# Memory attention and a one-expert MoE on one core: column sums as eight small products, a maximum in pieces, looser holds for VectorE's steps, the last tile in halves, smaller transfers

## The chip, the cores and the metric

One core of one Trainium2 chip. The metric is the device time of one execution, in microseconds (us), as the median of the runs shown. Engines: PE is TensorE (PEld its weight loads), DVE is VectorE, ACT is ScalarE, POOL is GpSimd, SP is SyncE, which here does nothing but issue DMAs. SPq and ACTq are the DMA issues on the queues of SP and ACT.

## The reference

```python
# q, k, v: (8, 8, 576, 64); phi: (8, 8, 576, 32)
a = softmax(phi, axis=2)                        # over the 576 tokens
k_m, v_m = a^T @ k, a^T @ v                     # (b, h, 32, 64)
attn = softmax(q @ k_m^T / 8)                   # over the 32 memories
x = (attn @ v_m), heads side by side            # (4608, 512)
logits = x @ w_gate + modality_bias[modality_id]
e = argmax(logits); g = softmax(logits)[e]
out = g * (relu(x @ w1[e]) @ w2[e])             # 8 experts, 512 -> 1024 -> 512
```

## The kernel before

The kernel guesses that all tokens go to one expert (the preferred one of the first token's bias), works everything out for that expert and checks the guess at the end; only if a token belongs elsewhere does a slow path run (it does not here). The 576 tokens of each of 8 batches are laid out as 64 rows by 9 columns; heads stand in two groups (`NG`) of four (`HG`).

For each batch b there is an attention part and an expert part.

The attention part, by its stage names: `max` (the maximum of phi over the 9 columns, on VectorE: `fold`, four operations that halve the width, for batches 1 to 7; a reduction over a strided view, L306, for batch 0), `top` (the maximum over the partitions), `exp` (subtract on VectorE at L368, exponent on ScalarE), `sums` (the sum over the columns, on POOL for batches 1 to 7), `kv` (`kv_products`: 72 products of 64 by 32 tiles, L403, then at L408 one product of 128 by 128 that sums over the partitions of each group by means of the 0/1 matrix `sides`; then the division), `kvT` (turned), `qt` (four turns of q, L539, on VectorE), `s` (scores, L548; L566 for batch 0), then the steps `e` (the turn out of PSUM L593, maximum L597, subtract L599, exponent L601), `n` (sum L609, reciprocal, multiply L619, turn L625), `xu` and `x` (the softmax weights split into an upper and a lower part, xah/xbh on ScalarE and xal/xbl on VectorE, L659 and L662), `l` (logits, L679 and L684), `g` (gates, L698 to L708) and `others`. The steps are made for two parts: the first four columns (xa) and the other five (xb). For odd batches `a_split` also saves xa and xb to DRAM, for the slow path.

The expert part: `vw` (the values times w1, L732, split into vwh by ScalarE, L153, and vwl by VectorE, L154), `h` (the hidden layer: for each of 8 slices six products, L779, into one PSUM bank; then `relu`: hh on ScalarE, L792, and the remainder hl on VectorE, L796) and `o` (the output tiles: 24 products of 512 columns each, L816; then the gate on ScalarE, L829, into one of two buffers `ob`, and the store, L837 or L841). The kinds of the hidden stages are h0 (first part, 0.72 us of TensorE each), h1 and h3 (second part of even and of odd batches, 0.9 us).

PSUM has four banks `pe` in a ring, for `h`, `vw` and `o`, and two pairs for the attention part. A hidden product waits for the `hl` that read the bank four allocations earlier.

What order the work has on every engine is settled by `weave` while the program is built: it keeps two lists, attention and experts, each in a fixed order, and takes in turn the stage that is ready by a model of costs (`TAKES`: TensorE's time and a chain such as "D1.5 A0.7" for VectorE 1.5 us, then ScalarE 0.7; T is VectorE at a time when POOL must be idle). An attention stage also has a due value, and is not taken before the experts' `progress` has reached it. Progress counts an output stage of 0.69 us as 0.69, a hidden stage at 0.35 and `vw` at 0.5 of its time. `BATCH` is the progress of a batch, 30.9. An attention stage with VectorE work is moreover held until

```python
ra = max(ra, free["D"] - (HOLD[ex[0][1]] - work if ex and ex[0][1] in HOLD else 3.5))
```

where `free["D"]` is when the model has VectorE free and `work` what the stage adds: with the next expert stage of kind h0, h1 or h3 it is taken only once VectorE's backlog and its own work stay within `HOLD`, else within 3.5 us. The engines then run their queues in that order, each waiting on semaphores.

The first 25 us are written out by hand in `plan_first`, with products on zeros (`warm`, `nothing`) in some places. From there on, `plan_memory`, `plan_turns` and `plan_steps` put the attention stages of each batch in the list; the due values of batch b start at `at0 = (b - 1) * BATCH - AHEAD - EARLIER`.

All loads and stores go through SP's queue in the order of the program: keys and values of batch b+1 once batch b's `kv` has been issued (`more_keys`), q of batch b+2 after the scores of batch b, in 16 DMAs of 72 KB that are issued one at each hidden or output stage (`load_some`, L195).

## Time and profile before

| | |
|---|---|
| median of 3 runs | 389.69 us (389.62 to 389.97) |
| the profiled execution | 389.69 us |
| its span in the profile | 387.9 us |
| PE busy | 375.3 us (97%) |
| DVE busy | 244.7 us (63%) |
| ACT busy | 141.3 us (36%) |
| POOL busy | 45.8 us (12%) |
| DMA | 56.89 MB in 91307 packets |
| products for output tiles, L816 | 864, 116.3 + 112.4 + 110.3 us busy |
| products on small tiles for keys and values, L403 and L408 | 1008 and 14, 15.7 and 2.7 us busy |

Busy times of PE overlap, since matmuls are pipelined: the time from one start to the next is shorter than the duration of one. The rows of a timeline give the start, the duration (of a run of equal instructions from the first start to the last end), the engine and line, what is written and read, how many, and in brackets how long the engine sat idle before and what ended that.

### The profile page before, as it was taken

The numbers are of one execution on the slowest core, as the hardware profiler recorded it, in microseconds if no ns is written. First come the engines' busy times: TensorE is split into PE (matmuls) and PEld (weight loads), VectorE is DVE, ScalarE is ACT, GpSimd is POOL, SyncE is SP. The second block draws the span as 40 slices with busy tenths as digits, with TensorE's granted clock in tenths as the row PEclk, the third lists the DMA queues.
The fourth block names the chain that finished last, engine by engine and source line by source line (L and its number), as shares of the span: only waits on it lengthen the run. The fifth ranks groups of instructions, "written<-read, shape, count | busy, mean of one in ns | idle before, by whom it ended". The sixth has DMA issues, their size and how long they took to land.

```text
span 387.9 us, 9645 instructions
## 1 busy us (share of the span) xinstructions
PE 375.3 (97%) x3891; PEld 303.3 (78%) x3893; DVE 244.7 (63%) x613; ACT 141.3 (36%) x327; POOL 45.8 (12%) x116
## 2 busy tenths in 40 slices
PE   6899999999999999999999999999999999999993
PEld 3577976889779886788879887798868878698982
DVE  4787756895786389836786476864887467750400
ACT  2382524425234243433433334323443325241410
POOL 4347030023000400030000300003000200000000
PEclk9999999999999999999999999999999999999997
DMA  8998679875761397639712397614411011531111
GB/s 300 379 394 183 103 140 344 225 210 150 243 120 42 94 298 184 208 82 276 119 34 56 75 300 126 255 28 119 182 29 42 15 30 27 198 102 32 28 36 55
DMA packets 91307, 56.89 MB, mean 147 GB/s; under 512 B 69236, under 2 KB 74356, under 8 KB 91252
## 3 DMA queue, kind: packets, MB, share of 16 engines
q1 hardware_dynamic: 90976, 55.87, 51.4%
q8 instruction: 33, 0.54, 0.6%
q10 hardware_dynamic: 276, 0.30, 0.2%
q14 instruction: 22, 0.18, 0.2%
HBM read 37.28 MB, written 18.87 MB: 145 GB/s over the span
## 4 chain that ended last, share of the span: by engine, by line
PE 85%; DVE 4%; SPq 4%; DMA 3%; ACT 1%; issue 1%; ACTq 0%
PE pe L816 47%; PE pe L779 24%; PE pair L403 4%; PE pe L732 3%; DMA q_sb<-in_q_dram 3%; SPq L195 3%; PE pair L548 2%; PE pair L679 1%; SPq L178 1%; DVE vwl L154 1%; PE pair L148 1%; PE pair L732 1%; PE pair L408 1%; DVE xbl L662 0%; ACT ob L829 0%
## 5 line engine op out<-in xcount | busy, mean ns | idle before, releaser
L816 PE MATMUL pe<-w2h,hh 128*128 128x512 f32 x288 | 116.3, 404 | 0.0
L816 PE MATMUL pe<-w2h,hl 128*128 128x512 f32 x288 | 112.4, 390 | 0.0
L816 PE MATMUL pe<-w2l,hh 128*128 128x512 f32 x288 | 110.3, 391 | 0.0
L796 DVE SCALAR_TENSOR_TENSOR hl<-pe,hh 128x256 fp32r<-128x256 f32 (+2 forms) x158 | 58.3, 392 | 43.1 <-ACT hh L792 42.3
L816 PEld LDWEIGHTS pe<-w2h,hh 128*128 128x128 f32 x288 | 54.1, 188 | 19.8 <-issue 9.7
L792 ACT ACTIVATE hh<-pe 128x256 fp32r<-128x256 f32 (+2 forms) x158 | 53.4, 362 | 41.6 <-PE pe L779 41.2
L816 PEld LDWEIGHTS pe<-w2l,hh 128*128 128x128 f32 x288 | 54.0, 188 | 11.8
L816 PEld LDWEIGHTS pe<-w2h,hl 128*128 128x128 f32 x288 | 54.2, 188 | 9.6
L829 ACT ACTIVATE ob<-pe,gates 128x512 f32<-128x512 f32 x36 | 24.6, 687 | 73.4 <-PE pe L816 48.1
L779 PE MATMUL pe<-xbh,vwh 128*128 128x320 f32 x128 | 40.3, 315 | 0.1
L779 PE MATMUL pe<-xbh,vwl 128*128 128x320 f32 x128 | 39.6, 309 | 0.0
L779 PE MATMUL pe<-xbl,vwh 128*128 128x320 f32 x128 | 39.6, 309 | 0.0
L779 PE MATMUL pe<-xah,vwh 128*128 128x256 f32 x124 | 35.2, 287 | 1.5 <-DVE hl L796 0.7
L779 PE MATMUL pe<-xal,vwh 128*128 128x256 f32 x124 | 35.0, 284 | 0.3 <-DVE xal L662 0.3
L779 PE MATMUL pe<-xah,vwl 128*128 128x256 f32 x124 | 34.9, 283 | 0.0
L337 POOL COPY ts<-tm 32x4 f32<-32x4 f32 x24 | 4.8, 199 | 198.8 <-DVE tm L329 198.1
L779 PEld LDWEIGHTS pe<-xah,vwh 128*128 128x128 f32 x124 | 23.6, 191 | 4.2 <-ACT xah L648 1.6
L779 PEld LDWEIGHTS pe<-xbh,vwh 128*128 128x128 f32 x128 | 24.0, 188 | 1.7 <-issue 0.9
L779 PEld LDWEIGHTS pe<-xbl,vwh 128*128 128x128 f32 x128 | 24.1, 188 | 0.3
L779 PEld LDWEIGHTS pe<-xal,vwh 128*128 128x128 f32 x124 | 23.7, 191 | 0.8 <-DVE xal L662 0.5
L779 PEld LDWEIGHTS pe<-xbh,vwl 128*128 128x128 f32 x128 | 24.0, 188 | 0.0
L779 PEld LDWEIGHTS pe<-xah,vwl 128*128 128x128 f32 x124 | 23.7, 191 | 0.0
(173 smaller groups left out, 430.0 us busy)
## 6 DMA issues: line engine op xcount, KB each, us to landing
kv_sb<-in_k_dram SPq DMA_DIRECT2D x8, 1152.0 KB, 7.2
kv_sb<-in_v_dram SPq DMA_DIRECT2D x8, 1152.0 KB, 9.7
out_dram<-ob SPq DMA_DIRECT2D x64, 128.0 KB, 2.4
q_sb<-in_q_dram SPq DMA_DIRECT2D x112, 72.0 KB, 2.8
ph<-in_phi_dram SPq DMA_DIRECT2D x7, 576.0 KB, 4.3
raw<-in_moe_w_dram SPq DMA_DIRECT2D x2, 1024.0 KB, 6.4
raw<-in_moe_w_dram SPq DMA_DIRECT2D x1, 1280.0 KB, 10.2
out_dram<-ob SPq DMA_DIRECT2D x4, 256.0 KB, 2.1
```

What stands on the lines that cost most here:

```text
L148: nc.tensor.transpose(dst, src, ident[:rows, :rows])
L154: nc.vector.tensor_tensor(l, src, h.bitcast(F32), op=ALU.subtract)
L195: nc.sync.dma_start(*later.pop(0))
L337: nc.gpsimd.tensor_copy(ts_[BL * a:BL * (a + 1)], live["tm"][BL * o:BL * (o + 1)])
L403: nc.tensor.matmul(live["kvp"][M * j:M * (j + 1), g], lhsT=pe[half, j, c * M:(c + 1) * M], rhs=kv_sb[half, :, j, c * D:(c + 1) * D], start ...
L548: nc.tensor.matmul(sc[g][M * j:M * (j + 1), a, 0:QC * BL], lhsT=kvT[b][rows, 0, M * j:M * (j + 1)], rhs=qT[rows, j, a], start=True, stop=T ...
L732: nc.tensor.matmul(pvs[g][M * j:M * (j + 1), :], lhsT=vT[b][rows, j, :], rhs=raw1[rows, j, cols], start=True, stop=not more, tile_position ...
L779: nc.tensor.matmul(ph[:, 0:n], lhsT=(vl if k == 2 else vh)[:, g, cols], rhs=xl if k == 1 else xh, start=(g == k == 0), stop=(g == NG - 1 a ...
L792: nc.scalar.activation(hs[0][:, f, h0:h0 + p1 - p0], live["ph", f][:, p0:p1], AF.Relu)
L796: nc.vector.scalar_tensor_tensor(hl, live["ph", f][:, p0:p1], 0.0, hh.bitcast(F32), op0=ALU.max, op1=ALU.subtract)
L816: nc.tensor.matmul(po, lhsT=tile_columns(hl if n == 1 else hh, f, t), rhs=(w2l if n == 2 else w2h)[:, f, :], start=(f == n == 0), stop=(f ...
L829: nc.scalar.activation(ob, po, AF.Copy, scale=gate_of(b, t))
```

## The change

- Idle products: one before and two after the subtraction of batch 0's maximum go (1 of 1, 2 of 4), and three before the second group's hidden products (3 of 3).
- In `kv_products` the one product with `sides` becomes eight with a column of ones, on the same 64 by 32 tiles as the products before it; the two groups' sums then lie in two banks. `sides` and its four memsets go.
- The maximum of batch 1: instead of `fold`, a strided reduction of heads 0 and 1 (`m2`), put before batch 0's second scores, one of head 2 before the step `n` of batch 0's second part, and one of head 3 between `xu` and `x` of that part (`m1`).
- `HOLD` rises from 1.9, 2.4, 2.2 to 2.2, 3.0, 2.7. `EARLIER` is 0 instead of -4 for batch 3 (its steps fall due 4 earlier than before) and -6 instead of 0 for batch 7 (6 later).
- The very last output tile: its two halves of 256 columns go through ScalarE and VectorE into two buffers, and are stored by SP and by ACT.
- The loads of keys and values of batches 1 to 7 are made in two column halves each. The saved copies of xa and xb lie in DRAM column by column, so that each piece is 1 KB instead of 4 or 5 KB.

```diff
-    sides = const.tile([P, NG], F32, name="sides")
-    xa_dram = [[dram.tile([P, NG * RA * P], ...
-    xb_dram = [[dram.tile([P, NG * RB * P], ...
+    xa_dram = [[dram.tile([RA, P, NG * P], ...
+    xb_dram = [[dram.tile([RB, P, NG * P], ...
+    def flat(x, n):
+        return x.rearrange("p i g c x -> p (i g c x)").rearrange("p (n y) -> p n y", n=n)
     def load_kv(b, t):
-        nc.sync.dma_start(kv_sb[:, t], halves((k, v)[t], b))
+        src = halves((k, v)[t], b)
+        pieces = 2 if b else 1
+        for i in range(pieces):
+            cols = slice(i * (QC * D // pieces), (i + 1) * (QC * D // pieces))
+            nc.sync.dma_start(kv_sb[:, t, :, cols], src[:, :, cols])
+    def heads_max(b, js):
+        if js.start == 0:
+            live["top", b] = wk.tile([P, HG, M], F32, name="top")
+        src = phs[b].rearrange("p j (c m) -> p j m c", m=M)
+        nc.vector.tensor_reduce(live["top", b][:, js], src[:, js], axis=AX.X, op=ALU.max)
     def kv_products(b):
-        live["psum"] = pk[:, 0, 2 * D:2 * D + NG]
+        live["psum"] = pk[:, :, 2 * D]
...
-        nc.tensor.matmul(live["psum"], lhsT=sums.rearrange("p j m -> p (j m)"), rhs=sides, start=True, stop=True)
+        for j in range(HG):
+            for g in range(NG):
+                half = slice(QP * g, QP * (g + 1))
+                nc.tensor.matmul(
+                    pk[M * j:M * (j + 1), g, 2 * D:2 * D + 1], lhsT=sums[half, j], rhs=ones_c[half],
+                    start=True, stop=True, tile_position=(QP * g, M * j),
+                )
     def a_split(b, part, step=None):
...
-                nc.sync.dma_start(d.bitcast(F32), x.rearrange("p i g c x -> p (i g c x)").bitcast(F32))
+                nc.sync.dma_start(d.bitcast(F32).rearrange("n p x -> p n x"), flat(x, n).bitcast(F32))
     def store(b, t):
         def finish(po):
+            if b == B - 1 and t is None:
+                rows = out[S * (b - 1):S * (b + 1)].rearrange("(p c) d -> c p d", c=QC)[QC - 1]
+                first, second = slice(0, DM // 2), slice(DM // 2, DM)
+                obs = [wk.tile([P, DM], F32, name="ob", bufs=2)[:, 0:DM // 2] for _ in range(2)]
+                nc.scalar.activation(obs[0], po[:, first], AF.Copy, scale=gate_of(b, t))
+                nc.vector.tensor_scalar(obs[1], po[:, second], gate_of(b, t), None, op0=ALU.mult)
+                nc.sync.dma_start(rows[:, first], obs[0])
+                nc.scalar.dma_start(rows[:, second], obs[1])
+                return
# TAKES
+        "m1": (0.0, "D0.55"), "m2": (0.0, "D1.1"),
-        "kv": (2.6, "D0.4 A0.7"),
+        "kv": (2.5, "D0.4 A0.7"),
# plan_memory
-            ("max", [], mem_max, 0.0),
+            *((("max", [], mem_max, 0.0),) if b > 1 else ()),
# plan_first
-        nothing(1)
         add(("exp", 0), "first exp", [("top", 0)], mem_exp, 0)
-        nothing(4)
+        nothing(2)
...
         add(("n", 0, 0, 1, 1), "n2", [], first_weights, 1, 1)
-        nothing(3, "pe")
...
         turns(1, 1, 27.2)
+        add(("max", 1, 0), "m2", [], heads_max, 1, slice(0, 2), floor=26.5)
# plan_steps
+        if b == 0:
+            names = [x[0] for x in todo]
+            for j, before in ((3, ("x", 0, 1)), (2, ("n", 0, 1, 0))):
+                todo.insert(names.index(before), (("max", 1, j - 1), "m1", [], heads_max, (1, slice(j, j + 1))))
+            todo += [(("max", 1), "nothing", [("max", 1, 2)], lambda: None, ())]
...
-    AHEAD, EARLIER, SPREAD = (5.8, 5.0), {3: -4.0}, 0.55
+    AHEAD, EARLIER, SPREAD = (5.8, 5.0), {7: -6.0}, 0.55
-        HOLD = {"h0": 1.9, "h1": 2.4, "h3": 2.2}
+        HOLD = {"h0": 2.2, "h1": 3.0, "h3": 2.7}
```

## The prediction

> **What bounds the kernel now.** I read the page first, then the table of busy times by stretch, then the waits of TensorE, then the timeline around each wait.

> ```profile
> span 387.9 us, 9645 instructions
> PE 375.3 (97%) x3891; PEld 303.3 (78%) x3893; DVE 244.7 (63%) x613; ACT 141.3 (36%) x327; POOL 45.8 (12%) x116
> ...
> 0.00:10.00 10.00, 7.03 (x141) 3.73 (x146) 4.82 (x11) 3.03 (x6) 4.04 (x34) 1.00 0.83 303
> 10.00:20.00 10.00, 8.80 (x253) 5.49 (x244) 7.97 (x26) 3.14 (x11) 2.94 (x13) 1.00 1.08 380
> 20.00:30.00 10.00, 9.69 (x92) 7.91 (x90) 8.31 (x20) 9.36 (x23) 4.79 (x4) 1.00 1.05 395
> 168.00:380.00 212.00, 212.00 (x1982) 174.04 (x1981) 122.16 (x308) 73.60 (x174) 14.82 (x31) 1.00 0.37 101
> ```

> The columns after the stretch are its length, then PE, PEld, DVE, ACT, POOL, the granted clock, the DMA share and GB/s. TensorE bounds the kernel: from 168 us to 380 us it has no gap at all, at full clock, so there only work taken from TensorE itself can shorten the run. Idle TensorE lies in the first 30 us (2.97+1.20+0.31 = 4.5 us), in the tail, and at two places between, which the waits name and the timeline of TensorE shows:

> ```profile
> 67.65 0.39 PE L779 MATMUL pe<-xah,vwh 128*128 128x256 f32 x1 [0.46 <-ACT xah L659]
> 68.38 0.39 PE L779 MATMUL pe<-xal,vwh 128*128 128x256 f32 x1 [0.34 <-DVE xal L662]
> 163.06 0.39 PE L779 MATMUL pe<-xah,vwh 128*128 128x256 f32 x1 [0.74 <-DVE hl L796]
> ```

> The bracket is the idle time just before and what ended it: a hidden product (L779) waits 0.80 us for batch 1's split of the weights and 0.74 us for VectorE's `hl` of batch 3. The sum below is made against the profiled execution, 389.69 us: 387.9 us of span and 1.79 us around it. It equals the median of the three runs.

> **Idle products.** One, two and three products of 512 columns go.

> ```profile
> 9.26 2.19 PE L422 MATMUL pair<-kv_sb,exp 64*64 64x128 f32 x72
> 23.09 0.50 PE L779 MATMUL pe<-xah,vwh 128*128 128x256 f32 x2 [0.26 <-ACT xah L648]
> 11.17 0.29 DVE L385 TENSOR_TENSOR sums<-sums,t2top 128x128 f32<-128x128 f32 x1
> 12.74 0.71 DVE L539 STREAM_TRANSPOSE q_sb<-q_sb 128x512 f32<-128x512 f32 x1 [0.31 <-DMA q_sb<-in_q_dram]
> ```

> The one stands before L361, which waits for VectorE anyway. The two stand before the first keys (9.26 to 11.45 us); an earlier start there ends at VectorE's sums all the same (11.46 us), and behind those the DVE queue stands until q has landed (12.74 us). The three stand before L779 at 23.09 us, which waits for ScalarE's xah even with them. All six: 0; at best -0.2 us if the keys' start counts (9.26 back to about 9.1, when the first exponents are there). If the idling lowered the clock, the products from 23.09 to 27.5 us would take twice as long, over 4 us; but the rows above grant 1.00 through 4.5 us of idling, so this gets 0.02, within rival 2. The four memsets of `sides` go from POOL, which waits for the token ids' load behind them: 0.

> **Sums as eight products.** For batches 1 to 7 the 128 by 128 product L408 becomes eight of 64 by 32, each issued as two instructions (L403's 72 products are 144 instructions).

> ```profile
> 131.84 2.25 PE L403 MATMUL pair<-kv_sb,exp 64*32 64x128 f32 x144
> 134.01 0.38 PE L408 MATMUL pair<-sides,sums 128*128 128x2 f32 x2
> 134.26 0.48 PE L816 MATMUL pe<-w2h,hh 128*128 128x512 f32 x1
> L403 PE MATMUL pair<-kv_sb,exp 64*32 64x128 f32 x1008 | 15.7, 271 | 0.0
> L433 PE MATMUL pair<-ones_c,sums x8: 193/204/214, 11.5 to 11.6; 64*64 64x1 f32 x8
> 11.51 0.29 PE L433 MATMUL pair<-ones_c,sums 64*64 64x1 f32 x8
> ```

> L408 holds TensorE from 134.01 to 134.26: 0.25 us. L403's last instruction starts at 131.84+2.25-0.27 = 133.82, so its 144 stand 13.8 ns apart, and 0.19 us go by before L408, a change of tile shape. That change stays, only later: the gain is small. The new instructions resemble L433 most (f32, one column): eight in 0.29 us less one of 0.204 us, so 12.3 ns apart; sixteen are 0.20 us. The shape change then follows an instruction of 204 instead of 271 ns and should be shorter by up to 0.07 us. Per batch 0.05 to 0.12 us; I take 0.08, times 7: **-0.55**. Bounds: at L403's 13.8 ns with an unchanged gap -0.2; at half of L433's spacing, as eight tiles share the array where it has four, and with the shorter gap -1.5. A loss would need over 16 ns apart. [...]

> **Maximum of batch 1 in pieces.** The fold's four operations go, three reductions come.

> ```profile
> 42.17 0.66 DVE L294 TENSOR_TENSOR t2top<-ph 128x512 f32<-128x512 f32 x1
> 43.65 0.29 DVE L298 TENSOR_TENSOR top<-top,ph 128x128 f32<-128x128 f32 x1
> L306 DVE TENSOR_REDUCE top<-ph 128x64 f32<-128x576 f32 x2 | 2.2, 1118 | 4.5 <-DMA ph<-in_phi_dram 4.5
> 31.15 0.91 DVE L593 STREAM_TRANSPOSE a<-pair 128x320 f32<-128x320 f32 x2 [1.85 <-PE pair L566]
> 35.56 0.82 DVE L609 TENSOR_REDUCE sa<-a 128x20 f32<-128x640 f32 x1 [0.73 <-ACT a L601]
> 39.55 0.82 DVE L662 TENSOR_TENSOR xbl<-aT,xbh 128x640 fp32r<-128x640 f32 x1 [0.85 <-ACT xbh L659]
> ```

> The fold takes 42.17 to 43.94, 1.77 us between the gates of batch 0 and the first `hl` of its second part. By L306 two heads cost 1.12 us and one head 0.56 (half). The pair stands before the scores of 31 us, where DVE idles 1.85 us; the two single ones stand before L609 and L662, where it idles 0.73 and 0.85 us for ScalarE. All three are covered. What they add is a need: phi of batch 1 by about 29 us.

> ```profile
> L175 SPq DMA_DIRECT2D ph<-in_phi_dram x7: 373/392/1452, 17.3 to 216.3; - x7
> DMA to landing us min/median/max: 3.7/4.1/10.0
> ```

> Issued at 17.3 with at most 10.0 us to land: 27.3 us. If it were later, the piece would hold up the `hl` behind it on DVE.

> **VectorE's work held back later (HOLD), and due times.** A step waits until VectorE's backlog plus the step is below HOLD. In the second part of batch 0 the planner's backlog after each h1 stage is 0.45+0.52 = 0.97 us, and the exponent step's VectorE cost 1.5: 2.47, over 2.4 and under 3.0. So today that step stands behind all eight `hl`, and after the change among them.

> ```profile
> 49.66 1.41 DVE L368 TENSOR_TENSOR exp<-ph,pair 128x640 f32<-128x640 f32 x2
> 60.89 0.78 DVE L593 STREAM_TRANSPOSE a<-pair 128x256 f32<-128x256 f32 x2 [3.19 <-PE pair L548]
> ```

> With the fold gone and the hold raised, L368 can run at about 46 us instead of 49.66; then come ScalarE's exponent, POOL's sums, keys and values, scores: L593 at about 57 instead of 60.89, and xah and xal 3 to 4 us before L779 asks for them. The two waits (0.46+0.34) go: **-0.80**. Next late there is nothing that I see: the values' weights are made on TensorE right before, and their remainder is wanted only by the fifth hidden product.

> ```profile
> 156.51 1.29 DVE L154 TENSOR_TENSOR vwl<-pe,vwh 128x512 fp32r<-128x512 f32 x2 [1.74 <-ACT vwh L153]
> 160.88 0.68 DVE L294 TENSOR_TENSOR t2top<-ph 128x512 f32<-128x512 f32 x1
> 162.59 1.41 DVE L796 SCALAR_TENSOR_TENSOR hl<-pe,hh 128x256 fp32r<-128x256 f32 x4
> ```

> At 162 us VectorE has had no pause since 156.5: L154, logits, split, gates of batch 3, then the maximum of batch 4, and only then the first `hl`; the fifth hidden product has no bank. The change lets batch 3 fall due 4 units earlier, about 4 us of output products, so its gates end before L154; the maximum alone (1.8 us), begun before the first hidden product, is over when the first `hl` could run. **-0.74**. Bounds for both waits: 0 to -1.54.

> What this costs: HOLD goes to the planner's own limit. Four banks of h0 last 4x0.72 = 2.88 us, less `hl` 0.45 and 0.1: 2.33, against 2.2 now. And it charges 0.7 us for the values' remainder where L154 takes 1.29: 0.6 too little, right before h0. Batch 7 falls due 6 later, and today VectorE has 0.67 us of idle left before that batch's first `hl`:

> ```profile
> 342.29 0.42 DVE L796 SCALAR_TENSOR_TENSOR hl<-pe,hh 128x256 fp32r<-128x256 f32 x1 [0.67 <-ACT hh L792]
> ```

> A small wait at one of the seven h0 stages is likely: **+0.3** (0 to 3.5).

> **Last tile.** ScalarE's 512 columns become 256 on each of two engines, with a store from each of two queues.

> ```profile
> 381.54 0.69 ACT L829 ACTIVATE ob<-pe,gates 128x512 f32<-128x512 f32 x1 [4.75 <-PE pe L816]
> 382.25 0.35 SPq L837 DMA_DIRECT2D out_dram<-ob  x1
> 0.73 0.48 ACTq L1204 DMA_DIRECT2D ph<-in_phi_dram  x1
> ```

> 256 columns from PSUM take 0.42 (the `hl` row above), so the stores start 0.27 us sooner; ScalarE's queue needs 0.48 to issue where SP's needs 0.35. **-0.2** (-0.35 to +0.1).

> **Smaller loads and stores.** Keys and values of batches 1 to 7 go as two DMAs each, 14 more issues on SP (28 DMAs for 14), and the saved splits in 1 KB instead of 4 or 5 KB pieces.

> ```profile
> 39.69 12.76 SPq L195 DMA_DIRECT2D q_sb<-in_q_dram  x18
> 52.56 2.87 SPq L841 DMA_DIRECT2D out_dram<-ob  x4
> 57.93 0.69 ACT L829 ACTIVATE ob<-pe,gates 128x512 f32<-128x512 f32 x1
> L178 SPq DMA_DIRECT2D kv_sb<-in_v_dram x8: 498/503/1670, 1.7 to 268.0; - x8
> ```

> SP is full from 39.69 to 55.4 us, and the outputs' first stores (52.56) stand behind its loads of q; the third output tile (57.93) needs their buffer. Two more issues of 0.5 us move the stores by 1 us; 52.56+1+2.87 = 56.4 still ends before 57.93. No wait of TensorE names a DMA. **0** (to +1, if the cover of about 1.5 us is used up).

> **Sum.** -0.55-0.80-0.74+0.3-0.2 = -2.0: **387.7 us**.

> **Rivals.** (1) The waits move rather than go: a backlog like that of 162 us comes back at another h0 stage, since HOLD is looser by 0.3 to 0.6. For it: the mischarged 0.6 us; against: four of the h0 stages after 168 us run without a gap. One wait of 0.7 and one of 0.5 instead of +0.3: 388.6 to 389.2. (2) Slower: VectorE becomes the bound in the h0 stages. A first `hl` up to about 1.0 us late costs nothing: the one at 162.59 could have run at about 160.9, when its products and ScalarE's part were done; it came 1.7 us late and TensorE lost 0.74. Each 0.1 us beyond costs as much. With the 0.6 at seven stages and the looser hold, 0.5 us each: 7x0.5 less 2.3 from the other terms gives 390.9; it decides from 0.33 us a stage. Against it: today VectorE still idles 0.67 us at 342. (3) The small products don't overlap as L433's do: at twice its spacing, 24.6 ns, sixteen take 0.39 us, 0.14 more than L408, and seven batches lose 1.0 in place of the 0.55 gained: 389.2. For it: eight tiles of 32 columns share the array where L433 has four of 64; against it: L403 has those eight tiles at 13.8 ns. [...]

> **How the numbers follow.** Forecast 0.62 (own range 386.3 to 388.5: below, all better bounds, -1.5-1.54-0.35 and no new wait; above, half of the waits' gain lost); rival 1 0.18, rival 2 0.14, rival 3 0.06. 0.2% is 0.78 us, about what a measurement can tell: faster is below 388.91. Forecast and half of rival 1 make 0.71 faster; the other half, rival 3 and a seventh of rival 2 make 0.17 same; the rest 0.12 slower. The range reaches over rivals 1 and 3 and leaves rival 2 out: 386.3 to 389.5.

> **What would show it.** No wait of L779 on xah, xal near 65 us and none on `hl` near 162; L368 for batch 1 among the `hl` at 45 to 47 us; from the last L403 product to the next full product 0.05 to 0.12 us less; TensorE's first product of 256 columns with new weights still at 23.1; the last ScalarE piece 0.4 us. Wrong if TensorE's waits on `hl` at h0 stages sum to over 1 us, if phi of batch 1 lands after 29 us, or if the sums' instructions stand over 16 ns apart.

## The result, and the profile after

The change made the kernel slower: 394.3 us median of 4 runs (392.98 to 395.57) against 389.65 (389.57 to 389.97), a ratio of 1.0117 (95% interval 1.0072 to 1.0163). The forecast was 387.7. The four runs fall into two pairs, 393 us with mean clocks of 0.997 and 0.996, and 395.5 us with 0.991 and 0.986; the profiled run, 393.13 us, is one of the first pair.

The page of the changed kernel:

```profile
span 391.0 us, 9857 instructions
PE 375.8 (96%) x3984; PEld 301.9 (77%) x3985; DVE 245.1 (63%) x613; ACT 140.6 (36%) x327; POOL 45.7 (12%) x112
...
q8 instruction: 33, 0.54, 0.6%
```

TensorE is as busy as before (375.8 against 375.3 us), so 2.6 of the 3.1 us of longer span are time in which it does nothing. Its list of waits (what it waited for, us in total, times, longest) has two that the kernel before did not have:

```profile
PE pe L794 <- issue: 1.6, 1, 1.6
...
PE pe L831 <- issue: 0.7, 1, 0.7
PE pair L147 <- DVE keys L481: 0.7, 1, 0.7
```

"Issue" means that no semaphore held it. The chain of the work that ended last shows where (start, length, what):

```profile
87.86 2.08 PE pair L412 x138
89.94 0.13 PE pair L420 x14
90.08 1.96 PE pe L794 x12
92.03 0.22 PE pair L147 x2
92.25 0.59 PE pe L794 x4
92.84 1.60 issue
94.44 3.19 PE pe L794 x20
...
172.19 2.08 PE pair L412 x138
174.27 0.13 PE pair L420 x14
174.41 0.67 PE pe L831 x2
175.08 0.72 issue
```

Both follow a batch's stretch of small products, keys and values (L412) and the new sums (L420). The stretch itself became shorter; in the chain of before it was 2.18+0.31 = 2.49 us, now it is 2.21:

```profile
171.66 2.18 PE pair L403 x144
173.84 0.31 PE pair L408 x2
174.16 1.50 PE pe L816 x6
```

Of TensorE's waits before, those at 67.65, 68.38 and 163.06 us are gone. The timeline of the changed kernel's TensorE at these places has no bracket, and VectorE's part of batch 1's exponents stands among the `hl` (46.64 against 49.66):

```profile
68.17 0.39 PE L794 MATMUL pe<-xah,vwh 128*128 128x256 f32 x1
...
161.49 0.28 PE L794 MATMUL pe<-xah,vwh 128*128 128x256 f32 x1
...
46.64 1.41 DVE L377 TENSOR_TENSOR exp<-ph,pair 128x640 f32<-128x640 f32 x2
```

And the start is late. The load of the first queries, on the chain of both, took 10.43 us before (from 2.29) and takes 0.58 us longer now, though nothing ahead of it was changed:

```profile
2.29 11.01 DMA q_sb<-in_q_dram
```

### The profile page after: what moved, and what is told of

It reads as the page before. It is cut to its first block, busy times and chain, and to the rows that moved or that the text cites. A ratio compares the mean times of both kernels' runs of the same rounds, so it can differ in the third digit from the quotient of the medians.

```text
span 391.0 us, 9857 instructions
## 1 busy us (share of the span) xinstructions
PE 375.8 (96%) x3984; PEld 301.9 (77%) x3985; DVE 245.1 (63%) x613; ACT 140.6 (36%) x327; POOL 45.7 (12%) x112
## 4 chain that ended last, share of the span: by engine, by line
PE 92%; DMA 3%; DVE 2%; issue 1%; ACT 0%; SPq 0%; ACTq 0%
PE pe L831 53%; PE pe L794 26%; PE pair L412 4%; PE pe L747 4%; DMA q_sb<-in_q_dram 3%; PE pair L563 2%; PE pair L694 1%; PE pair L581 1%; PE pair L147 1%; PE pair L543 0%; SPq L184 0%; DVE aT L657 0%; PE pair L420 0%; DVE a L653 0%; DVE mx L612 0%
## 5 line engine op out<-in xcount | busy, mean ns | idle before, releaser
L811 DVE SCALAR_TENSOR_TENSOR hl<-pe,hh 128x256 fp32r<-128x256 f32 (+2 forms) x158 | 57.5, 389 | 40.4 <-ACT hh L807 39.3
L831 PEld LDWEIGHTS pe<-w2h,hh 128*128 128x128 f32 x288 | 54.0, 188 | 23.3 <-issue 13.2
L152 ACT CAST vwh<-pe 128x512 fp32r<-128x512 f32 x26 | 14.0, 590 | 31.3 <-PE pe L747 31.3
L794 PEld LDWEIGHTS pe<-xal,vwh 128*128 128x128 f32 x124 | 23.7, 192 | 0.2
```

The costliest lines, as they stand in the source:

```text
L152: nc.scalar.copy(h, src)
L794: nc.tensor.matmul(ph[:, 0:n], lhsT=(vl if k == 2 else vh)[:, g, cols], rhs=xl if k == 1 else xh, start=(g == k == 0), stop=(g == NG - 1 a ...
L811: nc.vector.scalar_tensor_tensor(hl, live["ph", f][:, p0:p1], 0.0, hh.bitcast(F32), op0=ALU.max, op1=ALU.subtract)
L831: nc.tensor.matmul(po, lhsT=tile_columns(hl if n == 1 else hh, f, t), rhs=(w2l if n == 2 else w2h)[:, f, :], start=(f == n == 0), stop=(f ...
```

## The experiments

Times are medians of 5 to 12 runs; the ratio, with its 95% interval, is to runs of the kernel before made beside them on the same chip. The table stands in four blocks of four rows, and the medians of the kernel before beside them were 389.92, 390.13, 390.00 and 389.88 us. A cost in us is a ratio, or a difference of two, times 390.

| kernel | us | ratio to before |
|---|---|---|
| x1_idle: changed, idle products back | 393.65 | 1.0113 (1.0085 to 1.0141) |
| x2_tail: changed, last tile whole | 392.08 | 1.0051 (1.0034 to 1.0068) |
| x3_whole: changed, whole loads and stores | 391.34 | 1.0034 (1.0022 to 1.0047) |
| x4_order: changed, order of before | 394.74 | 1.0118 (1.0099 to 1.0136) |
| y1_sums: before + small sums | 392.72 | 1.0075 (1.0058 to 1.0091) |
| y2_order: before + new order | 389.27 | 0.9978 (0.9969 to 0.9986) |
| y3_both: before + both (seven runs; an eighth took 2066.48 us) | 392.35 | 1.0056 (1.0034 to 1.0078) |
| z_shift: changed, 126 instructions more at the start | 392.05 | 1.0053 (1.0036 to 1.0071) |
| p1_pad: y3_both + column kept | 391.0 | 1.0021 (1.0003 to 1.0040) |
| p2_split: p1_pad + stretch cut in two | 388.9 | 0.9974 (0.9961 to 0.9986) |
| t1_tail: y2_order + halves | 389.95 | 1.0002 (0.9989 to 1.0014) |
| t2_pieces: y2_order + pieces | 389.71 | 0.9989 (0.9980 to 0.9998) |
| a1_column: changed, column kept | 391.21 | 1.0029 (1.0013 to 1.0044) |
| a2_split: changed, stretch cut | 391.12 | 1.0032 (1.0019 to 1.0045) |
| a3_both: changed, both repairs | 389.4 | 0.9999 (0.9983 to 1.0016) |
| c1_moved: y2_order + one column | 390.32 | 1.0010 (1.0000 to 1.0019) |

**Undoing one part at a time.** x1_idle puts the six idle products back:

```diff
+        nothing(1)
         add(("exp", 0), "first exp", [("top", 0)], mem_exp, 0)
-        nothing(2)
+        nothing(4)
...
+        nothing(3, "pe")
```

> The changed kernel with the six idle products put back. The four times of the changed kernel fall into two groups, 393.0 and 395.5 us, and the granted clock into two, 0.997 and 0.986 to 0.991; the kernel before shows 0.994 and one group. Theory A (the idling after the removed products lets the clock fall in some executions): all times near 393, clock 0.994 or more. Rival B (the two groups come from the transfers): still two groups. In both, the hidden products of the second group begin near 23.1 to 23.7 us, since the trace of the changed kernel has them wait for xah.

No change that can be told from 394.3, and the times still spread, from 393.17 to 396.65 us: the idle products are not the cause.

x2_tail goes back to one tile and one store at the end (the `if b == B - 1 and t is None` block of `store` is taken out):

> The changed kernel with the old last tile: one gate on ScalarE, one store from SP. In the trace of the changed kernel the two halves ran one after the other, and from the last product's end to the end of the span went 7.6 us instead of 6.45, with 0.35 us more around the span. Theory A (the second queue and the serial halves cost): 1.2 to 1.5 us less than the changed kernel in each of its groups, the tail back to 6.45. Rival B (the tail is longer because of what lies before it): no change.

Faster than the changed kernel by some 2 us, with runs from 390.97 to 393.03; the spread hides what the tail itself costs (t1_tail below).

x3_whole takes back the pieces:

```diff
-        pieces = 2 if b else 1
+        pieces = 1
...
-    xa_dram = [[dram.tile([RA, P, NG * P], F32R, ...
+    xa_dram = [[dram.tile([P, NG * RA * P], F32R, ...
```

> The changed kernel with keys and values loaded whole and xa, xb saved in 4 and 5 KB pieces again. In the trace of the changed kernel TensorE stands still for 1.6 us at 92.8 and for 0.7 us at 175.1 with no semaphore to wait for, a transfer of instructions on its way in both windows and the DMA engines full with the kernel's own small pieces. Theory A (the small pieces delay the instructions): both gone, 2.3 us less, and SP's queue of q loads ends near 52 instead of 56.5 us. Rival B (the new order puts the dense stretch of small products next to a busy queue whatever the pieces): the standstills stay, within 0.5 us of the changed kernel.

391.34, and all runs within 0.7 us. Its trace has both standstills still, of 0.40 us at 92.81 and 0.91 us at 173.67.

x4_order undoes the maximum in pieces, HOLD and the due times:

> The changed kernel with the order of before: HOLD, due times and batch 1's maximum as they were. Theory A (the order gains its two waits, 1.5 us, and the loss is in the tail, the transfers and the clock): 0 to 1.5 us slower than the changed kernel, waits of L779's place on xah, xal near 68 and on hl near 163 back. Rival B (VectorE's looser hold is the loss): 2 us or more faster than the changed kernel.

No better, so the order is not the loss. Its trace (a run of 396.26 us) shows a second cost. TensorE stands for 2.13 us from 95.69, nine products into the sums, and then (columns: stretch, length, PE, PEld, DVE, ACT, POOL, granted clock, DMA share, GB/s):

```profile
95.90:97.70 1.80, 0.00 (x0) 0.00 (x0) 0.00 (x0) 0.00 (x0) 0.00 (x0) 1.00 0.74 166
97.90:99.10 1.20, 1.20 (x13) 1.19 (x14) 0.95 (x4) 0.54 (x2) 0.00 (x0) 1.00 1.05 375
99.20:102.50 3.30, 3.30 (x12) 2.90 (x11) 2.39 (x7) 1.26 (x5) 0.00 (x0) 0.50 1.10 364
102.60:105.00 2.40, 2.40 (x25) 1.50 (x30) 0.53 (x1) 0.00 (x0) 0.00 (x0) 1.00 0.37 123
```

The clock falls to a half for one period, 99.16 to 102.57 by the trace's clock records, 3.41 us: 12 products run in it, and at half speed about 1.7 us of work is lost once more, an estimate (half of 3.41). y3_both shows the same after a standstill of 1.96 us (half clock from 96.04, 3.41 us), while 1.89 us at 93.3 in x2_tail left the clock whole. Every period of clock that ends inside one of the traces is a multiple of 3.41 us: the full clock lasts 378.88 us in the kernel before and 382.29 us in the changed one, 111 and 112 times 3.413. Cut into such periods from the times in the clock records, TensorE stood for 2.07 us of one in x4_order and 1.96 us of one in y3_both, and the next was at half clock; in x2_tail the standstill lay across two (0.96 and 0.94 us), and in x1_idle 1.78 us of one period left the next whole. That the idle time within one such period decides would fit these four traces; nothing further shows it. Both traces with the drop also have a half-speed period near 17 us (17.24 and 17.53, 3.41 us each), ahead of any standstill. A low mean clock thus does not tell where the clock fell, nor what it cost: a run of x2_tail at 0.990 took 390.97 us, the least of its eight.

**Where TensorE stands.** I counted the matmuls and weight loads that the traces show before each standstill. In the changed kernel, the four above, y1_sums, y3_both, p1_pad and a1_column the first standstill comes after 2464 to 2468 of them and the second after 4235 to 4237, at times from 91.3 to 95.7 and 173.1 to 179.2 us. These are other products in x1_idle, where the restored ones put 11 records in front, and in x4_order, where the order differs. So the place follows the count, not the work; the difference, about 1770, is seven times 253. The trace has 33 transfers of 16 KB on the queue named "instruction" (0.54 MB), about one per 250 records, and in the changed kernel seven lie from the one that lands at 93.18 us, at the first standstill, to the one at 174.51 us, at the second. I call what one of them brings a block. In all twenty standstills of these traces such a transfer lands 1.2 to 1.5 us before TensorE goes on. The first of the changed kernel:

```profile
q1 hardware_dynamic: 197, 0.26, 95.5%
q8 instruction: 1, 0.02, 4.6%
```

These are the queues of the changed kernel from 92 to 93.3 us (packets, MB, share). This block arrives from 92.22 to 93.18; TensorE goes on at 94.44. Since the transfer before it, 524 records had run, more than two blocks; elsewhere it is mostly 90 to 400. The stretch of one batch is 320 records in 2.2 us, 1.3 blocks. A reading that fits: if a block ends early in the stretch, the next one ends a few instructions behind it, and the transfer asked for at the first end is late. What asks for a transfer, and when, no trace shows. Counted on by 252.7 (the 1769 records between the two standstills of y1_sums, by seven), block ends lie 103 and 70 records into the stretches of batches 2 and 4 of the changed kernel; in batches 1, 3, 5, 6 and 7 at 183, -25, 117, -47 and -36. Most such ends cost nothing: the changed kernel has 33 transfers and two standstills. The longest standstill is 2.13 us (x4_order).

z_shift tests this by moving the count alone:

```diff
-    BUSY = 92, 10
+    BUSY = 156, 9
```

> The changed kernel with 64 more small idle products and one large one fewer, all while TensorE waits for the first queries; it computes the same and only moves every later product 126 instructions down the stream, so that other products stand at the ends of the 16 KB blocks. Theory A: the standstills at 92.8 us (1.6) and 175.1 us (0.7) are gone, since the block ends move from 103 and 70 instructions behind the start of the kv stretches of batches 2 and 4 to -23 and -56; shorter ones may come in behind the stretches of batches 1 and 3, whose ends now lie at 57 and 102. Time 391 to 393, against 394.3. Theory B (full queues and pieces at that time hold TensorE up, whatever instruction it is at): both standstills stay at these places with 1.6 and 0.7 us and the time stays at 393 to 395.6.

The chain of z_shift, batches 1 and 2:

```profile
52.51 2.08 PE pair L412 x138
54.59 0.10 PE pair L420 x10
54.69 1.53 issue
56.23 0.22 PE pair L420 x3
...
91.33 2.08 PE pair L412 x138
93.41 0.13 PE pair L420 x13
93.55 1.95 PE pe L794 x12
95.50 0.22 PE pair L147 x2
95.72 3.37 PE pe L794 x23
```

Both old standstills are gone, and one of 1.53 us has come up in batch 1, whose block now ends 57 records in. Batches 3, 6 and 7 (102, 80 and 91 records by the same count) did not stand, so the place of a block's end does not decide alone; what else does is not shown. The standstills move with the count of instructions and end 1.2 to 1.5 us after a block's landing, so I take the instruction supply for their cause; full queues alone are not.

**Parts alone.** Three kernels built up from before:

> The kernel before with one thing of the change: the sums of the weights as sixteen small products a batch instead of one large one. Theory A (TensorE's instructions come in blocks of 16 KB; where a block ends inside or just behind the 320 small instructions of a batch's kv stretch and the next block, about 253 instructions on, ends within some 40 instructions of the stretch's end, the next block lands too late and TensorE stands; how long goes by how full the DMA queues are): the stretch falls from 2.42 to 2.22 us, -0.20 by seven batches = -1.4, and one or two standstills without a semaphore come in, in batches 2 and 4, together 0.5 to 2 us, less than in the changed kernel since transfers are whole here; time 389 to 390.3. Theory B (the standstills come from the loads and stores in smaller pieces alone): no standstill, time 388.3 to 388.7. My prediction's term for this part alone was -0.55: 389.3.

> The kernel before with the order alone: maximum of batch 1 in pieces, VectorE's work held back later, the later due time moved from batch 3 to batch 7. The prediction's own terms for these are -0.80 (waits at 67.65 and 68.38 us) -0.74 (wait at 163.06) +0.3 (batch 7) = -1.24: 388.6. Theory A: both waits gone as in the changed kernel; no new standstill, since the stretch of small products keeps its 292 instructions and 2.42 us, unless a block end falls in it in batch 3 (0 to 0.5 us); more switches between tile shapes take some 0.3 back: 388.2 to 389.2. Rival C (putting the changed kernel's order back did not make it faster, so the order gains nothing): 389.7 to 390.2.

> The kernel before with both: sums as small products and the new order, but whole loads and stores, the last tile in one, and the six idle products kept. Theory A: gains of -1.4 (sums) and -1.5 (waits) against before, less 1.3 us of standstills in batches 2 and 4 (0.40 and 0.91 in the changed kernel with whole transfers, whose stream of products this is but for 11 instructions): 388 to 389.2, faster than before. Theory B: no standstill: 387 to 387.6. Rival C: no better than 389.7. If the late landing of the first queries (13.3 instead of 12.7 us in the changed kernel) comes from the sums or the order, it shows here as well and adds 0.6.

y2_order is faster than before by 0.9 us, without a standstill: the waits' gain is real. y1_sums costs 2.9 us, with standstills of 0.50 at 95.48 and 1.23 at 175.65; I had expected no loss even with them. Whole transfers do not prevent it: in y3_both they are 1.96 and 1.59. Of the 3.1 us by which y1_sums' profiled span is longer than before's, 1.73 are the standstills, 0.74 a later start (the hidden products after the first queries at 23.83 instead of 23.09 us), 0.63 a wait for batch 1's keys at 59.8 us and 0.6 the tail; the shorter stretches take 1.3 back, and 0.7 I could not place. The late start sorts the kernels: the first queries land at 13.2 to 13.5 us in the seven kernels so far that have small sums and their queries' load on the chain, at 12.7 us in y2_order.

**The column.** The table `sides` (8 bytes in each partition), which only the large sum read, went with it. p1_pad allocates and fills it again:

```diff
     places = const.tile([P, 2], F32, name="places")
+    sides = const.tile([P, NG], F32, name="sides")
```

> The kernel before with sums as small products and the new order (as y3_both), and the old table of two columns that the large sum read (sides) kept in memory and still filled, though nothing reads it. Theory D (without this 8-byte column every later tile lies at another address, and transfers into them run slower: packets of 1024 bytes took 49.5 ns against 46.0 and the first queries landed at 13.4 instead of 12.7 us in all five kernels without it): the first queries land at 12.7 us, packets of 1024 bytes take 46.0 ns, and all that follows comes 0.6 us earlier than in y3_both; its fastest run 390.59 becomes about 390.0, and its profile shows standstills at the same instructions (2468 and 4237 of TensorE's stream). Rival E (the late landing has to do with the small products themselves or with the code's length): 13.4 us and 49.5 ns stay.

The queries' load takes 10.4 us again, and the 512 packets of 1024 bytes in the first 13 us take 46.0 ns on average (by the packet records) as before. So they do in all eight kernels that keep the table and add no tile; in the nine that dropped it they take 49.4 to 49.7. c1_moved makes the shift without small sums, by one more unused tile in y2_order:

```diff
     sides = const.tile([P, NG], F32, name="sides")
+    spare = const.tile([P, 2], F32, name="spare")
```

> The kernel before with the new order (y2_order, 389.27) and one more unused column of 8 bytes behind the table sides; sums stay one large product, no instruction changes, all later tiles lie 8 bytes (or the allocator's grain) higher. If an address off its old grain slows transfers whichever way it is off: first queries at 13.3 us, 1024-byte packets at 49.5 ns, 389.8 to 390.1. If only the missing column does it, or something else of the sums: 12.7 us, 46.0 ns, 389.2 to 389.4.

49.7 ns, queries late, and 1.2 us slower than y2_order (1.0010 against 0.9978, times 390). Of the 1.56 us by which its profiled span is longer, 0.48 are the queries' load and 0.74 lie behind the start of the last product; I could not place the rest. The chain of c1_moved:

```profile
2.29 10.92 DMA q_sb<-in_q_dram
```

So I put it down to where the later tiles lie; the traces hold no addresses. Which grain counts was not tried.

**The cut.** p2_split lets five of the nine groups of key and value products run first and the rest with the sums later, in batches 2 and 4, and keeps the table unfilled:

```diff
-        for c in range(QC):
+        for c in some:
...
-        kv_products(b)
+        kv_products(b, range(KVA, QC) if b in (2, 4) else range(QC))
```

> As p1_pad, but the table is only kept and not filled, and in batches 2 and 4 the stretch of 320 small instructions is cut in two of 160 with some 4 us of full products (24 in batch 2, 15 in batch 4) between them; the number of TensorE's instructions stays. Theory A (a 16 KB block that ends too soon behind the one before it lands too late): the second block's end comes some 4 us later than in y3_both, so the standstills of 1.96 and 1.59 us fall to 0 to 0.5 each, and the clock stays whole; cost of four more changes of tile shape 0.2 to 0.5 us. Time 387.5 to 389, faster than before and than y2_order. Without theory A (full queues hold TensorE up whatever it runs): 390 to 393. If the address and not the filling makes the late landing (theory D), the first queries land at 12.7 us here as well.

Its chain in batch 2:

```profile
87.06 1.30 PE pair L408 x80
88.36 3.72 PE pe L797 x24
92.08 0.99 PE pair L408 x58
93.07 0.13 PE pair L418 x14
93.20 1.95 PE pe L797 x12
95.16 0.22 PE pair L148 x2
```

No standstill there or in batch 4, the clock whole, queries at 12.7 although the table is not filled, and 388.9 us: 1.0 us faster than before and, by medians, 0.4 less than y2_order, which the intervals don't tell apart. It beats both kernels.

**Halves and pieces alone**, on y2_order:

> The kernel before with the new order (y2_order, 389.27) and the last tile in halves, nothing else. My prediction's term for the halves was -0.2 (-0.35 to +0.1): 389.1. By the trace of the changed kernel, where the second half's copy began 0.03 us behind the end of the first (0.47 then 0.48) and the time from the last product's start to the span's end rose from 6.45 to 7.6 us, and what lies outside the span from 1.8 to 2.15: +1.2 to +1.6, 390.5 to 390.9.

The halves cost 0.9 us (1.0002 against 0.9978). ScalarE, VectorE and the two issuing queues at the end of t1_tail, then of y2_order:

```profile
381.20 0.47 ACT L841 ACTIVATE ob<-pe,gates 128x256 f32<-128x256 f32 x1 [4.75 <-PE pe L819]
381.70 0.34 SPq L843 DMA_DIRECT2D out_dram<-ob  x1
381.71 0.48 DVE L842 TENSOR_SCALAR ob<-pe,gates 128x256 f32<-128x256 f32 x1 [15.75 <-ACT ob L841]
382.22 0.38 ACTq L844 DMA_DIRECT2D out_dram<-ob  x1
```

```profile
381.16 0.69 ACT L832 ACTIVATE ob<-pe,gates 128x512 f32<-128x512 f32 x1 [4.75 <-PE pe L819]
381.87 0.34 SPq L840 DMA_DIRECT2D out_dram<-ob  x1
```

VectorE waits for ScalarE's half, so the last store is issued at 382.22 instead of 381.87, 0.35 us later. Another 0.37 us lies outside the span (2.18 against 1.81 us, medians of all runs); what that is stays open, since a2_split and a3_both have the halves and 1.8 us.

> The kernel before with the new order (y2_order, 389.27), k and v of batches 1 to 7 loaded in two pieces and the weights stored and fetched in smaller pieces, nothing else; sums stay one large product. My prediction's term was 0 (up to +1): 389.3. Theory A (pieces matter only by making the queues fuller when a block of instructions ends in a dense stretch, and the stretch of 292 here had no standstill): 389.1 to 389.6. Theory B (pieces cost by themselves, as 394.3 against 391.34 of the changed kernel without them suggests): 390.5 to 392.

+0.4 us by themselves, without a standstill.

**Repairing the changed kernel.**

> The changed kernel with the unused 8-byte column kept in memory (not filled). Theory (the column's absence moves all later tiles and slows transfers): first queries land at 12.7 instead of 13.3 us, 1024-byte packets take 46.0 instead of 49.6 ns, 0.6 us earlier throughout; the standstills at instructions 2465 and 4234 stay (1 to 2 us each) and with them the spread: 392.3 to 393.8 against 394.3. If the column does not matter once the transfers are in pieces: 394.3.

> The changed kernel with the kv stretch of batches 2 and 4 cut in two, with 24 and 15 full products between. Theory: no standstill over 0.5 us at instructions 2465 and 4234, the clock whole in every run, the spread of the runs under 1 us; the 0.6 us at the start stays: 390.3 to 391.5 against 394.3. If the pieces hold TensorE up by themselves, standstills stay somewhere near 90 and 175 us and the time is 392 to 395.

> The changed kernel with both repairs: column kept, stretch cut in two in batches 2 and 4. If the two causes and the parts measured alone add up: p2_split's 388.9 and 0.65 for the last tile in halves and 0.45 for the pieces = 390.0, range 389.6 to 390.6, about the time before. Anything over 391 means that a part of the loss is still not found.

With the column kept, batch 2's standstill fell from 1.60 to 0.23 us, while batch 4's rose from 0.72 to 1.24. With the stretch cut and the column gone, one standstill is left, at record 2465 again, now inside the second half:

```profile
93.93 0.07 PE pair L424 x8
94.00 0.79 issue
94.79 0.24 PE pair L424 x7
```

I had expected none over 0.5 us, a whole clock in every run and a spread under 1 us; a2_split's runs spread over 1.6 us, and three of the eight have mean clocks of 0.990 or 0.991. Of the three repaired kernels only a3_both has no standstill.

With both repairs the changed kernel runs in 389.4 us, no different from before (0.9999). The parts added up to 390.0, which its interval (389.2 to 390.5) allows; less than that cannot be told. Each repair alone takes away 3 us, more than I had given the column, and both together 4.6, so they overlap. That slower transfers delay the blocks too would fit, but one trace of each does not show it.

## Why the prediction was wrong

**Sums: -0.55, measured +2.9.** This is the step that failed. The gain on the products themselves was even underrated: from the chain, 2.49 to 2.21 us a batch, less 0.09 that the twelve hidden products behind it take longer (1.96 us above, 1.87 in the chain of y2_order below), is -0.19, times 7 -1.3, inside the bounds (-0.2 to -1.5). The spacing, taken as 12.3 ns from L433, nearly held too: in the timeline of the changed kernel the sixteen instructions take 0.22 us to the next product's start, under 14 ns each.

```profile
89.78 0.29 PE L420 MATMUL pair<-ones_c,sums 64*32 64x1 f32 x16
90.00 0.42 PE L794 MATMUL pe<-xbh,vwh 128*128 128x320 f32 x1
```

```profile
87.30 2.18 PE pair L406 x144
89.47 0.31 PE pair L411 x2
89.79 1.87 PE pe L782 x12
```

What the step left out were two effects that lie in no instruction's duration. It priced the removal of `sides` by its memsets (0) and not by where the tiles behind it come to lie. And it took packing 320 instructions into 2.2 us for free, though the page shows the 33 instruction transfers; TensorE then stood for its own instructions (1.73 us in y1_sums, 2.32 us in the changed kernel), at a place that depends on the count of all instructions before. With both effects out (p2_split) the gain over y2_order is some 0.2 to 0.4 us, with the cut paid for.

**Loads and stores in pieces: 0 (to +1), alone +0.4.** Inside the range, but only where nothing else is short. In the changed kernel they cost 3.2 us (1.0117 against 1.0034). Longer standstills are 1.0 of it in the two traces (2.32 against 1.31 us); the rest is not placed. A busy queue does go with a late block: counted from the block end before, 253 records back, TensorE went on 2.4 us later where the kernel's own transfers took 3% of the DMA engines (y1_sums, batch 2; over the standstill and the 2.5 us ahead of it), 3.1 to 3.7 us later at 33 to 63%, 4.1 at 77%, and 4.6 to 6.3 above 90%. But whole transfers fill the queues there as well: y3_both, which has them, stood for 3.55 us. In this I argued from "no wait of TensorE names a DMA"; the wait that came has no name.

**Last tile: -0.2 (-0.35 to +0.1), measured +0.9.** The step assumed that both engines read the tile at once. The first store does go 0.17 us sooner (381.70 against 381.87), but the halves run one behind the other, held by a semaphore: ScalarE's ends at 381.67 us and VectorE's starts at 381.71. Why the program has that semaphore was not shown.

**Maximum in pieces, HOLD and due times: -0.80, -0.74, +0.3, together -1.24; measured -0.9** (-1.2 to -0.5). Right in the mechanism, with 0.4 us less than the sum: no wait on `xah`, `xal` or `hl` at those places, the exponents at 46.64. phi of batch 1 was just in time: issued at 18.6 us instead of 17.3, it took 10.4 us to land, and its first piece started at 29.53.

**Idle products: 0.** Right as far as 1.0113 against 1.0117 can tell, with intervals of over 1 us to each side.

**The rivals.** VectorE as the bound did not come: `hl` is not in TensorE's list of waits. Nor did slow small products. The case that came true, that TensorE waits for its own instructions, was none of them, and so the chance of slower, 0.12, stood on the wrong mechanism.

Not shown: whether the changed kernel's clock fell after a standstill as in x4_order and y3_both. The mean clocks of 0.991 and 0.986 in two of its runs would fit half-speed periods, but in the one profiled the clock stayed whole from 6.4 to 388.7 us.

## What to carry to other kernels

Cutting time per instruction was not free here, where it packed 320 records, 1.3 blocks, into 2.2 us and the traces show standstills of 0.23 to 2.13 us. Over such a stretch, look at the instruction queue's transfers and count how many instructions ran between them. If a part of an edit measures far from its instruction's prices, test the layout (one unused column) and the count (idle instructions in front) before blaming the edit. And a removed tile can be a change to every tile behind it: here the packets of 1024 bytes went from 46.0 to 49.7 ns.
